# A convolution plus a feed-forward layer on one core: two short tiled matmul steps set in one run, and a third step set in pairs

## The chip, the cores and the metric

The kernel runs on one core of one Trainium2 chip, in float32 and in float32 split into two rounded parts. The metric is the time of one execution in microseconds on the device. The kernel before was timed in three runs, with a median of 1113.24 us.

## The reference, cut to what matters

```python
xn = layernorm(x)                       # x: 2048 positions x 576 channels
# branch A: a long convolution along the positions, one response per channel
P = exp(dt * A * l)                     # l = 0..2047, 128 complex modes per channel
K = real(sum_n C[d,n] * P[d,n,l] * dt[d] * B[d,n])     # the response of channel d
y = irfft(rfft(pad(xn.T)) * rfft(pad(K)))[:2048] + xn * Dskip
# branch B: a feed-forward layer, 576 -> 4608 -> 576
h = silu(xn @ w1)
out = x + y.T + h @ w2
```

The convolution is done as a transform of length 2048 in steps (radix 32, then 64): a first step for the inputs `xn`, the same first step for the responses `K`, a product in the middle, and the way back.

## The kernel before, in words

One generator, `ffn`, issues the feed-forward layer, which is most of TensorE's work: `up` (L313 to L315, tile `ph`) multiplies by `w1`, ScalarE applies silu (`gf`, L321) and rounds (`gh`, L322), VectorE takes the remainder (`gl`, L323); `down` (L338, tile `po`) multiplies by `w2`, and VectorE adds the result to `acc` (L342). Each product is three matmuls of rounded parts.

A second generator, `side`, issues the convolution. `weave` puts its pieces between those of `ffn`: each piece yields a mark, a share of the whole, at which it is due. Within that, a scheduler orders every engine's instructions at build time by priorities, dependencies and free buffers, and the engines then run these fixed orders.

The change is in the stretch of `side` in which the responses are computed (`kgen`, marks 0.13 to 0.597), and the inputs' first step (`spread`) runs beside it.

- `kgen` has 36 chunks of channels. For each, VectorE and ScalarE make tables of sines and cosines (`S`, `C`). At every second chunk a pair is complete. Then TensorE sums the modes into `kp` by 64 small matmuls (L674) which use the array as four column strips of 128x32; ScalarE copies `kp` to `kt` (L681); and TensorE does the first transform step of the same pair by eight matmuls into the two tiles `z` (L689), which use the array as two halves of 64x128. ScalarE copies them into `stage` (L697), and every two pairs SP's queue stores `stage` to `d1k` (L702).
- `spread` has 16 groups of positions and two steps in each. SP's queue loads a group into `xr` (L145). A step rounds half of the rows on ScalarE (`sp`, L150), takes the remainder on VectorE (L151), and does four full 128x128 matmuls in two tiles `pu` (L155, L156), which ScalarE copies to `u1` (L157). POOL's queue stores it to `d1u` (L158). The pool `up` has one buffer of each tile. `side` calls one step after every chunk from the third on.
- `kp`, the two `z` and the `pu` tiles take turns in three PSUM buffers of the pool `pss`.

POOL's queue also loads the later tiles of the feed-forward's input (`xl`, L352; `r4`, L355). After `kgen` an accumulating DMA adds `Dskip` to `d1k` (L705), and the spectral stage (`front`, tiles `pk`, `pu`, `pb`, L804) loads `d1u` and `d1k` (L796).

Of the kernel before, what the change touches and what calls it, by code (L numbers as in the profile page):

```python
# [11 lines left out]
F32 = mybir.dt.float32  # L12
# [7 lines left out]
P = 128  # L20
# [23 lines left out]
def kernel(  # L44
# [21 lines left out]
    nc = tc.nc  # L66
# [14 lines left out]
    d1k = dram.tile([32 * P, D], F32, name="d1k")  # L81
    d2 = dram.tile([32 * P, D], F32, name="d2")
    dxt = [dram.tile([D, 512], F32, name=f"dxt{b}") for b in range(2)]
    dxn = dram.tile([P, NJ, D], F32, name="dxn")
# [6 lines left out]
    f1 = cst.tile([P, P], F32, name="f1")  # L91
# [18 lines left out]
    pss = ctx.enter_context(tc.tile_pool(name="pss", bufs=3, space=PSUM))  # L110
# [25 lines left out]
    def behind(ins):  # L136
        return tc.issue_after(ins) if ins is not None else nullcontext()

    def spread(up):

        s1 = up.tile([P, 2, P], F32R, name="s1", bufs=1)
        nc.gpsimd.dma_start(s1, cs1)
        for j in range(NJ):
            src = up.tile([P, D], F32, tag="xr", name="xr")
            nc.sync.dma_start(src, dxn[:, j])  # L145
            for m in range(2):
                lo, hi = slice(64 * m, 64 * m + 64), slice(64 - 64 * m, 128 - 64 * m)
                u1 = up.tile([P, D], F32, tag="u1", name="u1")
                sp = up.tile([P, D], F32R, tag="sp", name="sp")
                nc.scalar.copy(sp[lo, :], src[lo, :])  # L150
                nc.vector.tensor_sub(sp[hi, :], src[lo, :], sp[lo, :])  # L151
                for h in range(2):
                    hs = slice(h * HD, (h + 1) * HD)
                    pu = pss.tile([P, 512], F32, tag="pss", name="pu")
                    nc.tensor.matmul(pu[:, :HD], s1[:, 0, :], sp[:, hs], start=True, stop=False)  # L155
                    nc.tensor.matmul(pu[:, :HD], s1[:, 1, :], sp[:, hs], start=False, stop=True)  # L156
                    nc.scalar.copy(u1[:, hs], pu[:, :HD])  # L157
                nc.gpsimd.dma_start(  # L158
                    d1u.rearrange("(p m j) d -> m j p d", m=2, j=NJ)[m, j], u1)
                yield j  # L160
# [401 lines left out]
    def kgen():  # L562
        fT, phiT = kf["f"], kf["phi"]
        with tc.tile_pool(name="kg", bufs=1) as kg:
            CH = 8
            NRUN = 4
            NCK = HD // CH
# [50 lines left out]
                return th  # L618

            stage = None  # L620
            tabs = []
            nxt = head(0)
            al = powers(0)
            for i in range(NCK):
                th = nxt
                pk, ak = pw[:, i % 2], al[:, :, i % 2]
                c65 = kg.tile([P, W, 65], F32, tag="c65", name="c65")
                S = kg.tile([P, W, 96], F32, tag="S", name="S", bufs=2)
                C = kg.tile([P, W, 96], F32, tag="C", name="C", bufs=2)
                mag = C  # L630
                nc.scalar.activation(c65, th, AF.Identity, bias=magic)  # L631
                nc.vector.scalar_tensor_tensor(th, c65, MAGIC, th, op0=ALU.subtract, op1=ALU.subtract)  # L632
                nc.scalar.activation(c65, th, AF.Abs)  # L633
                nc.scalar.activation(th, th, AF.Sin, scale=TWO_PI)
                nc.scalar.activation(c65, c65, AF.Sin, scale=-TWO_PI, bias=halfpi)
                for g in range(2):
                    gs = slice(g * CH, (g + 1) * CH)
                    nc.vector.tensor_mul(
                        mag[:, gs, 0:32].rearrange("n d (x y) -> n d x y", y=4),
                        pk[:, gs, 0, :].unsqueeze(3).broadcast_to([P, CH, 8, 4]),  # L640
                        ak[:, g].unsqueeze(2).broadcast_to([P, CH, 8, 4]))
                nc.vector.tensor_mul(
                    mag[:, :, 32:96].rearrange("n d (x y) -> n d x y", y=8),
                    pk[:, :, 1, :].unsqueeze(3).broadcast_to([P, W, 8, 8]),
                    pk[:, :, 2, :].unsqueeze(2).broadcast_to([P, W, 8, 8]))
                if i + 1 < NCK:
                    nxt = head(i + 1)
                    if i % 2 == 1:
                        al = powers(i + 1)
                for dst, t, sg in ((S, th, -1.0), (C, c65, 1.0)):  # L650
                    ov3 = dst.rearrange("n d (x y) -> n d x y", y=32)[:, :, 0:3:2, :]
                    mv3 = mag.rearrange("n d (x y) -> n d x y", y=32)[:, :, 0:3:2, :]
                    nc.vector.tensor_mul(ov3, t[:, :, 0:64].rearrange("n d (x y) -> n d x y", y=32), mv3)
                    nc.vector.scalar_tensor_tensor(dst[:, :, 32:64], t[:, :, 64:32:-1], sg, mag[:, :, 32:64],  # L654
                                                   op0=ALU.mult, op1=ALU.mult)
                tabs.append((S, C))
                if i % 2 == 0:
                    yield (i + 1) / NCK
                    continue

                kp = pss.tile([P, 512], F32, tag="pss", name="kp")
                first = None
                for e in (1, 0):
                    S, C = tabs[e]
                    for gl in range(2):
                        for gp_ in range(2):
                            o = e * 256 + (gl * 2 + gp_) * 64
                            for q in range(4):
                                ch = gp_ * CH + gl * 4 + q
                                dst = kp[32 * q:32 * q + 32, o:o + 64]  # L670
                                begins = e == 1 and gl == 0 and gp_ == 0
                                with tc.high_priority(), behind(None if begins else first):
                                    for n, t in enumerate((C, S)):
                                        mm = nc.tensor.matmul(dst, t[:, ch, :32], t[:, ch, 32:],  # L674
                                                              start=begins and n == 0, stop=True,
                                                              tile_position=(0, 32 * q), skip_group_check=True)
                                if begins:
                                    first = mm.ins
                tabs = []
                kt = kg.tile([P, 512], F32, tag="kt", name="kt")  # L680
                nc.scalar.copy(kt, kp)  # L681

                z = [pss.tile([P, 512], F32, tag="pss", name="z") for _ in range(2)]
                first = None
                for eg in range(4):
                    for h in (1, 0):
                        rows = slice(64 * h, 64 * h + 64)
                        with tc.high_priority(), behind(first):
                            mm = nc.tensor.matmul(z[h][:, eg * P:(eg + 1) * P], kt[rows, eg * P:(eg + 1) * P], f1[rows],  # L689
                                                  start=True, stop=True, tile_position=(64 * h, 0))  # L690
                        first = first or mm.ins
                r = (i - 1) % NRUN
                if r == 0:
                    stage = kg.tile([P, 64, NRUN * CH], F32, tag="stage", name="stage")
                sv = stage[:, :, r * CH:(r + 2) * CH].rearrange("p k (e h c) -> p h e k c", h=2, c=2)
                for h in range(2):
                    nc.scalar.copy(sv[:, h], z[h].rearrange("p (e k c) -> p e k c", e=4, c=2))  # L697
                if r == NRUN - 2:
                    d0 = (i // NRUN) * NRUN * CH
                    kv = d1k.rearrange("(k n) (g d) -> g n k d", n=64, g=2)  # L700
                    for gp_ in range(2):
                        nc.sync.dma_start(kv[gp_, :, :, d0:d0 + NRUN * CH], stage[gp_ * 64:(gp_ + 1) * 64])  # L702
                yield (i + 1) / NCK

        nc.gpsimd.dma_start(d1k.rearrange("(k n) d -> n k d", n=P)[0],  # L705
# [135 lines left out]
    def side():  # L841
# [3 lines left out]
        with tc.tile_pool(name="kf", bufs=1) as kfp:  # L845
# [50 lines left out]
            with tc.tile_pool(name="up", bufs=1) as up:  # L896
                sp = spread(up)
                for n, at in enumerate(kgen()):
                    if n > 1:
                        next(sp, None)  # L900
                    yield marks[0] + at * (marks[1] - marks[0])
                for _ in sp:
                    pass
# [8 lines left out]
        yield from tail()  # L912

    sd = side()
    fg = ffn()
    for g in (sd, fg, sd, sd, fg, sd, fg, sd):
# [84 lines left out]
```

## Time and profile before

| | us |
|---|---|
| median of three runs | 1113.24 (1112.6 to 1115.7) |
| the profiled execution, its own time | 1113.42 |
| its span, first to last instruction | 1111.6 |
| TensorE matmul busy | 1103.3 |
| VectorE busy | 916.9 |
| ScalarE busy | 709.2 |
| GpSimd busy | 69.8 |

The granted TensorE clock was full throughout. In the views, PE is TensorE's matmuls, PEld its weight loads, DVE is VectorE, ACT is ScalarE, POOL is GpSimd and SP the engine that issues most DMAs; a q behind a name is the engine's sequencer or DMA queue. An f32 matmul is recorded twice in the trace, so that a run of 64 matmuls shows as 128 records. In a timeline the first column is the start and the second the duration; matmuls overlap, so that the pitch, from one start to the next, is what a matmul takes of TensorE's time.

### The profile page before, as it was taken

The numbers are of one execution on the slowest core, as the hardware profiler recorded it, in microseconds if no ns is written. First come the engines' busy times: TensorE is split into PE (matmuls) and PEld (weight loads), VectorE is DVE, ScalarE is ACT, GpSimd is POOL, SyncE is SP. The second block draws the span as 40 slices with busy tenths as digits, with TensorE's granted clock in tenths as the row PEclk, the third lists the DMA queues.
The fourth block names the chain that finished last, engine by engine and source line by source line (L and its number), as shares of the span: only waits on it lengthen the run. The fifth ranks groups of instructions, "written<-read, shape, count | busy, mean of one in ns | idle before, by whom it ended". The sixth has DMA issues, their size and how long they took to land.

```text
span 1111.6 us, 22913 instructions
## 1 busy us (share of the span) xinstructions
PE 1103.3 (99%) x9168; PEld 997.8 (90%) x9168; DVE 916.9 (82%) x1546; ACT 709.2 (64%) x1228; POOL 69.8 (6%) x129
## 2 busy tenths in 40 slices
PE   8999999999999999999999999999999999999998
PEld 6998999899889899899989989999999999999887
DVE  6899899999999999999999837787778778784433
ACT  5574456676777676677866536877777878773210
POOL 1100000000000000011000000000000000000111
PEclk9999999999999999999999999999999999999999
DMA  9745522425242515255844163554545445434983
GB/s 258 201 122 152 137 71 61 120 63 130 82 107 80 134 61 131 77 149 161 219 123 105 44 173 106 169 157 128 161 145 150 139 146 171 129 107 130 248 211 86
DMA packets 175563, 148.56 MB, mean 134 GB/s; under 512 B 111024, under 2 KB 142272, under 8 KB 175328
## 3 DMA queue, kind: packets, MB, share of 16 engines
q1 hardware_dynamic: 165136, 112.33, 38.7%
q0 software_dynamic: 9568, 33.62, 9.5%
q8 instruction: 72, 1.18, 0.5%
q10 hardware_dynamic: 752, 1.15, 0.4%
q14 instruction: 35, 0.29, 0.1%
HBM read 102.53 MB, written 44.61 MB: 132 GB/s over the span
## 4 chain that ended last, share of the span: by engine, by line
PE 97%; DMA 1%; DVE 0%; SPq 0%; issue 0%; ACT 0%; ACTq 0%; POOL 0%; DVEq 0%
PE po L338 42%; PE ph L313 35%; PE kp L674 3%; PE ph L314 3%; PE ph L315 3%; PE pu L804 2%; PE pb L804 2%; PE pk L804 2%; PE z L689 2%; PE pu L155 1%; DMA acc<-in_A_u_dram 1%; PE py L825 1%; PE pu L156 1%; DMA w2r<-in_B_w_dram 0%; PE pt L124 0%; DVE st L186 0%
## 5 line engine op out<-in xcount | busy, mean ns | idle before, releaser
L338 PE MATMUL po<-w2l,gh 128*128 128x288 f32 x1152 | 338.5, 295 | 0.9 <-DVE w2l L302 0.9
L338 PE MATMUL po<-w2h,gl 128*128 128x288 f32 x1152 | 336.2, 295 | 0.0
L338 PE MATMUL po<-w2h,gh 128*128 128x288 f32 x1152 | 335.8, 295 | 0.0
L338 PEld LDWEIGHTS po<-w2h,gh 128*128 128x128 f32 x1152 | 215.1, 188 | 7.6 <-issue 2.8
L338 PEld LDWEIGHTS po<-w2l,gh 128*128 128x128 f32 x1152 | 215.9, 188 | 6.1 <-DVE w2l L302 1.1
L338 PEld LDWEIGHTS po<-w2h,gl 128*128 128x128 f32 x1152 | 215.4, 188 | 0.8
L321 ACT ACTIVATE gf<-ph 128x512 f32<-128x512 f32 (+1 forms) x148 | 86.4, 585 | 142.9 <-PE ph L315 128.3
L313 PE MATMUL ph<-xh,w1h 128*128 128x512 f32 (+1 forms) x592 | 162.1, 388 | 1.2 <-ACT gf L321 1.2
L313 PE MATMUL ph<-xl,w1h 128*128 128x512 f32 (+1 forms) x592 | 161.4, 386 | 0.0
L313 PE MATMUL ph<-xh,w1l 128*128 128x512 f32 (+1 forms) x592 | 161.0, 385 | 0.0
L342 DVE TENSOR_TENSOR acc<-po,acc 128x288 f32<-128x288 f32 x288 | 126.4, 452 | 37.4 <-PE po L338 36.1
L323 DVE TENSOR_TENSOR gl<-gf,gh 128x512 fp32r<-128x512 f32 (+1 forms) x148 | 99.2, 673 | 64.8 <-ACT gh L322 64.1
L313 PEld LDWEIGHTS ph<-xh,w1l 128*128 128x128 f32 x592 | 108.1, 188 | 19.9
L313 PEld LDWEIGHTS ph<-xl,w1h 128*128 128x128 f32 x592 | 108.0, 188 | 20.0 <-DVE xl L126 0.2
L313 PEld LDWEIGHTS ph<-xh,w1h 128*128 128x128 f32 x592 | 104.5, 188 | 18.5 <-ACT gf L321 1.8
L322 ACT CAST gh<-gf 128x512 fp32r<-128x512 f32 (+1 forms) x148 | 89.8, 609 | 10.1 <-PE po L338 7.1
L631 ACT ACTIVATE c<-th,magic 128x1040 f32<-128x1040 f32 x36 | 42.1, 1169 | 37.9 <-DVE C L654 28.0
L633 ACT ACTIVATE c<-th 128x1040 f32<-128x1040 f32 x36 | 38.7, 1075 | 34.0 <-DVE th L632 34.0
L300 ACT CAST w2h<-w2r 128x576 fp32r<-128x576 f32 x72 | 46.9, 671 | 17.2 <-PE po L338 14.9
L282 DVE TENSOR_TENSOR w1l<-w1r,w1h 128x640 fp32r<-128x640 f32 x72 | 57.1, 818 | 0.2
L314 PE MATMUL ph<-x,w1h 128*128 128x512 f32 (+1 forms) x148 | 57.0, 385 | 0.0
L315 PE MATMUL ph<-x,w1l 128*128 128x512 f32 (+1 forms) x148 | 56.9, 385 | 0.0
(184 smaller groups left out, 1830.1 us busy)
## 6 DMA issues: line engine op xcount, KB each, us to landing
w2r<-in_B_w_dram SPq DMA_DIRECT2D x72, 288.0 KB, 3.7
w1r<-in_B_w_dram SPq DMA_DIRECT2D x35, 512.0 KB, 3.9
d1u<-u POOLq DMA_DIRECT2D x32, 288.0 KB, 2.6
d1k<-stage SPq DMA_DIRECT2D x18, 512.0 KB, 6.8
ur<-d1u SPq DMA_DIRECT2D x32, 288.0 KB, 3.9
kr<-d1k SPq DMA_DIRECT2D x32, 288.0 KB, 2.8
d<-yo POOLq DMA_DIRECT2D x32, 288.0 KB, 3.7
ys<-d SPq DMA_DIRECT2D x32, 288.0 KB, 11.6
```

The lines of the kernel that those rows point to most:

```text
L282: pins["w1l"] = nc.vector.tensor_sub(l1, src, h1).ins
L300: pins["w2h"] = nc.scalar.copy(h2, r2).ins
L313: nc.tensor.matmul(ph, w[:, kt, :], v[:, kt, a:e], start=n + kt == 0, stop=False)
L314: nc.tensor.matmul(ph, h1[:, 4, :], x4[:, a:e], start=False, stop=False)
L315: pins["pe"] = nc.tensor.matmul(ph, l1[:, 4, :], x4[:, a:e], start=False, stop=True).ins
L321: nc.scalar.activation(gf, ph, AF.Silu)
L322: pins["gh"] = nc.scalar.copy(gh, gf).ins
L323: pins["gl"] = nc.vector.tensor_sub(gl, gf, gh).ins
L338: pins["pe"] = nc.tensor.matmul(po[:, :HD], G[blk, t][g][:, js], W2[half, c, t][w][:, hs], start=n == 0, stop=n == 3 * FT - 1).ins
L342: nc.vector.tensor_add(acc[j][:, hs], po[:, :HD], acc[j][:, hs])
L631: nc.scalar.activation(c65, th, AF.Identity, bias=magic)
L804: nc.tensor.matmul(dst, st, mv[:, hs], start=n == 0, stop=n == 3 * len(terms) - 1)
```

## The change

The first transform step of a pair is taken out of the loop's body into a function, `along`, and is issued one pair later, straight behind the next pair's `kp` matmuls; the last pair's is issued at the end. `kt` gets two buffers, since it lives one pair longer. `spread` is called twice after every chunk of even number from the third on, that is after a chunk that makes tables alone, instead of once after each. The loads of `xr` go to POOL's queue instead of SP's.

```diff
         for j in range(NJ):
             src = up.tile([P, D], F32, tag="xr", name="xr")
-            nc.sync.dma_start(src, dxn[:, j])
+            nc.gpsimd.dma_start(src, dxn[:, j])
...
+            kts = []
+            def along(first):
+                nonlocal stage
+                i, kt = kts.pop(0)
+                z = [pss.tile([P, 512], F32, tag="pss", name="z") for _ in range(2)]
+                for eg in range(4):
+                    for h in (1, 0):
+                        rows = slice(64 * h, 64 * h + 64)
+                        with tc.high_priority(), behind(first):
+                            mm = nc.tensor.matmul(z[h][:, eg * P:(eg + 1) * P], kt[rows, eg * P:(eg + 1) * P], f1[rows],
+                                                  start=True, stop=True, tile_position=(64 * h, 0))
+                        first = first or mm.ins
+                ...
+                for h in range(2):
+                    nc.scalar.copy(sv[:, h], z[h].rearrange("p (e k c) -> p e k c", e=4, c=2))
+                ...
...
                 tabs = []
-                kt = kg.tile([P, 512], F32, tag="kt", name="kt")
+                if kts:
+                    along(mm.ins)
+                kt = kg.tile([P, 512], F32, tag="kt", name="kt", bufs=2)
                 nc.scalar.copy(kt, kp)
-                z = ...        # the same matmuls, copies and stores, for this pair's own kt
+                kts.append((i, kt))
+                if i + 1 == NCK:
+                    along(None)
                 yield (i + 1) / NCK
...
                 for n, at in enumerate(kgen()):
-                    if n > 1:
+                    if n % 2 == 0 and n:
+                        next(sp, None)
                         next(sp, None)
                     yield marks[0] + at * (marks[1] - marks[0])
```

More of the change, by code (lines that the diff above doesn't have):

```diff
@@ L620, in kgen @@
             stage = None
+            kts = []
[10 more added lines that the diff above has]
+                        first = first or mm.ins
+                r = (i - 1) % NRUN
+                if r == 0:
+                    stage = kg.tile([P, 64, NRUN * CH], F32, tag="stage", name="stage")
+                sv = stage[:, :, r * CH:(r + 2) * CH].rearrange("p k (e h c) -> p h e k c", h=2, c=2)
+                for h in range(2):
+                    nc.scalar.copy(sv[:, h], z[h].rearrange("p (e k c) -> p e k c", e=4, c=2))
+                if r == NRUN - 2:
+                    d0 = (i // NRUN) * NRUN * CH
+                    kv = d1k.rearrange("(k n) (g d) -> g n k d", n=64, g=2)
+                    for gp_ in range(2):
+                        nc.sync.dma_start(kv[gp_, :, :, d0:d0 + NRUN * CH], stage[gp_ * 64:(gp_ + 1) * 64])
             tabs = []
@@ L679, in kgen @@
                 tabs = []
-                kt = kg.tile([P, 512], F32, tag="kt", name="kt")
+                if kts:
+                    along(mm.ins)
+                kt = kg.tile([P, 512], F32, tag="kt", name="kt", bufs=2)
                 nc.scalar.copy(kt, kp)
[L683 to L702, printed above, removed]
+                kts.append((i, kt))
+                if i + 1 == NCK:
+                    along(None)
                 yield (i + 1) / NCK
```

## The prediction

> **What bounds the kernel now.** I read the page's totals first, then who TensorE waited for, then the stretch that the change touches.
>
> ```profile
> span 1111.6 us, 22913 instructions
> ...
> PE 1103.3 (99%) x9168; PEld 997.8 (90%) x9168; DVE 916.9 (82%) x1546; ACT 709.2 (64%) x1228; POOL 69.8 (6%) x129
> ...
> PE 97%; DMA 1%; DVE 0%; SPq 0%; issue 0%; ACT 0%; ACTq 0%; POOL 0%; DVEq 0%
> ```
>
> The first two lines are totals, the third the chain that ended last. TensorE is on the chain for 97% of the span. The next lines are everything that the matmuls waited for in the whole run, and then the busy time of the engines in the stretch of `kgen`.
>
> ```profile
> PE pz L857 <- DVE zero L852: 1.3, 1, 1.3
> PE ph L313 <- ACT gf L321: 1.2, 3, 0.5
> PE po L338 <- DVE w2l L302: 0.9, 1, 0.9
> PE pt L124 <- DVE xn L195: 0.2, 1, 0.2
> ```
>
> ```profile
> core 0: us, PE busy (x) PEld busy (x) DVE busy (x) ACT busy (x) POOL busy (x), PEclk, DMA share, GB/s
> 180.00:640.00 460.00, 460.00 (x4859) 415.67 (x4860) 441.98 (x661) 317.03 (x477) 21.53 (x39) 1.00 0.41 109
> ```
>
> Waits come to 3.6 us, none of them in this stretch: there PE is busy for 460.00 of 460.00 us at full clock. So nothing that other engines or queues save can show in the time here; only a shorter stream of matmuls can. DVE is busy for 441.98 of 460, close behind.
>
> Busy is not the same as useful, though. The starts of matmuls show what it costs to go between the full array, the four strips of `kp` and the two halves of `z`. First into and out of a run of `kp`, then of `z`:
>
> ```profile
> 169.88 0.29 PE L338 MATMUL po<-w2h,gh 128*128 128x288 f32 x1
> 170.01 0.29 PE L338 MATMUL po<-w2l,gh 128*128 128x288 f32 x1
> 170.23 0.27 PE L674 MATMUL kp<-C 128*32 128x64 f32 x3
> ...
> 172.07 0.22 PE L674 MATMUL kp<-S 128*32 128x64 f32 x1
> 172.22 0.54 PE L338 MATMUL po<-w2h,gl 128*128 128x288 f32 x2
> 172.60 0.29 PE L338 MATMUL po<-w2h,gh 128*128 128x288 f32 x1
> ```
>
> ```profile
> 177.15 0.39 PE L315 MATMUL ph<-x,w1l 128*128 128x512 f32 x1
> 177.37 0.39 PE L313 MATMUL ph<-xh,w1h 128*128 128x512 f32 x1
> 177.69 0.38 PE L689 MATMUL z<-f,kt 64*128 64x128 f32 x2
> ...
> 178.57 0.28 PE L689 MATMUL z<-f,kt 64*128 64x128 f32 x2
> 178.78 0.40 PE L155 MATMUL pu<-sp,s 128*128 128x288 f32 x1
> 179.02 0.30 PE L156 MATMUL pu<-sp,s 128*128 128x288 f32 x1
> ```
>
> A `po` follows a `po` after 0.13 us, but the first `kp` follows after 0.22: 0.09 more. From `ph`, 0.32 instead of 0.22 to 0.23: again 0.09. On the way out the first full matmul starts 0.15 behind the last `kp`, and the one behind it 0.11 late: 172.22 to 172.60 is 0.38 for two where 0.26 is usual, and directly at 178.78 to 179.02, 0.24 for 0.13. The first matmuls of `z` take 0.38 where its last take 0.28: 0.10 for a weight load that nothing hides.
>
> **The change, part by part.**
>
> *One run instead of two.* Before there are 18 runs of `kp` (1152 records of `C`, 64 to a run, and as many of `S`) and 18 of `z` (288, 16 to a run), with full matmuls between all of them:
>
> ```profile
> L674 PE MATMUL kp<-C 128*32 128x64 f32 x1152 | 35.2, 222 | 0.0
> ...
> L689 PE MATMUL z<-f,kt 64*128 64x128 f32 x288 | 20.9, 285 | 0.0
> ```
>
> In the changed program as built, 17 runs of `kp` are followed at once by the eight `z` matmuls of the pair before; the number of matmuls of each kind is the same. Two things are new: the last pair's `z` follows 9 `up` matmuls later and is cut into four and four, with 4 `up` matmuls between.
>
> For one merge, before: 0.15 out of `kp`, 0.11 for the late second matmul, and 0.09 into `z`, 0.35 us in all; after: one direct step from `kp` to `z`. No row of before shows that step. Its bounds are `kp`'s own pitch, as if nothing had to be switched (170.23 to 172.07 is 1.84 us for 127 steps: 0.015), and the 0.22 from `po` into `kp`. I take 0.15, from `kp` to `po`: the same run has to end, and what comes next is another division of the array in either case. A merge then saves 0.35 - 0.15 = 0.20 us (0.13 to 0.335), and 17 save 3.4 us (2.2 to 5.7). The unhidden first load of `z` stays, since it is inside the run.
>
> The Trainium skill, TensorEngine Tiling (Array Packing), section Tiling Modes, says that changing the mode, and not merely the tile, drains the engine. By that rule strips to halves drains as strips to full does, and the sum goes by 0.15; the 0.09 on every way in agrees with it, and no run of before shows strips to halves.
>
> The cut of the last `z` adds one way out and one way in: at the cut 0.20 (178.58 to 178.78) for a mean pitch of some 0.06 to 0.10, so +0.10; then 0.11, 0.09 and the 0.10 of a first load: +0.40 us.
>
> *ScalarE's copies behind the merged run.* A run now holds all three `pss` buffers, and the first `pu` after it needs one back.
>
> ```profile
> L681 ACT COPY kt<-kp x18: 561/572/588, 172.5 to 640.5; 128x512 f32<-128x512 f32 x18
> ```
>
> `kp`'s buffer comes free first, 0.57 us after ScalarE gets to it, while the `z` part of the run still takes 178.78 - 177.69 = 1.1 us. In the built order at least 14 full matmuls (2 `up`, 12 `down`: 2.0 us) stand between a run and the next `pu`. So ScalarE may be 1.1 + 2.0 - 0.6 = 2.5 us late at no cost; with ACT busy for 317 of 460 us I cost this at nothing. If that cover were gone it is paid once a run.
>
> *The steps of `spread` in pairs.* Their matmuls are full ones and keep their pitch wherever they stand. But `u1` has one buffer, so the second step's copy waits on ScalarE until the first step's store has landed. Behind it on ScalarE stand `gf` and `gh`, for which TensorE waits.
>
> ```profile
> L158 POOL DMA_DIRECT2D d1u<-u x32: 539/539/577, 183.8 to 628.3; - x32
> DMA to landing us min/median/max: 2.4/2.6/5.6
> ```
>
> In the built order ScalarE has 3.0 to 3.4 us of other work between the two steps' copies in three of the sixteen pairs, 4.0 to 4.4 in five, more in the others (before: 4.0 at least). That covers a landing of 2.6 us. Cost nothing; without the cover up to 5.6 - 3.0 = 2.6 us in a pair.
>
> *The loads on POOL's queue.*
>
> ```profile
> L145 SPq DMA_DIRECT2D xr<-dxn x16: 326/333/808, 137.1 to 583.4; - x16
> SPq L145 <- DVE sp L151: 76.9, 13, 11.8
> POOL xl L352 <- PE ph L313: 9.1, 2, 5.0
> L362 ACT CAST xh<-xl x8: 615/622/633, 506.2 to 546.1; 128x512 fp32r<-128x512 f32 x8
> ```
>
> SP loses 16 issues of 0.33 us and 76.9 us in which the weights' loads stood behind a load that waited for `sp`. As matmuls wait for no load in this stretch, the gain is nothing. POOL gains 16 issues of about 0.54 (as for `d1u`), 8.6 us beside 21.5 in the 460. A load waits for the second step's `sp` and stands ahead of that step's own store, which can't be ready earlier. The second load of `xl` gets one such load ahead of it; some 25 instructions of ScalarE lie between that and its first use at L362, so nothing again; at most a few us, once. A load that lands some 3 us after issue has most of a pair's time, (640 - 180)/16 = 29 us, ahead of its use.
>
> *The end of `kgen`.* The last `z` leads to the store, to the DMA that adds `Dskip`, to the loads of the spectral stage:
>
> ```profile
> 656.93 0.86 POOL L705 DMA_DIRECT2D d1k<-in_A_Dskip_dram  x1 [28.09 <-DMA d1k<-stage]
> 662.76 0.32 SPq L796 DMA_DIRECT2D kr<-d1k  x1
> 673.38 0.67 ACT L790 CAST kh<-kr 128x576 fp32r<-128x576 f32 x1
> 646.34 1.20 PE L313 MATMUL ph<-xh,w1h 128*128 128x512 f32 x4
> kr<-d1k SPq DMA_DIRECT2D x32, 288.0 KB, 2.8
> ```
>
> From the end of `z` (646.34) to landed data it took 662.76 + 2.8 - 646.34 = 19.2 us. In the built order 58 `up` and 107 `down` matmuls, 58 x 0.227 + 107 x 0.133 = 27.4 us, now lie between the last `z` and the first `pk` (79 and 100 before, 31.2 us). 8 us are left for the splits; nothing.
>
> **Sum.** -3.4 + 0.4 = -3.0 us against the profiled execution's own 1113.42 us, whose span is 1111.6: 1110.4. The median of the runs is 0.2 lower, so 1110.2 us, 0.27% less. A measurement of this kernel tells about 0.3%, 3.3 us, from no change: 1109.9 is the border.
>
> **Rivals.** *No switch from strips to halves.* At 0.015 a merge saves 0.335, in all 5.7 - 0.4 = 5.3 us: 1107.9. For it: both divide the array, and small matmuls follow each other at 0.015. Against: the drain on each way in.
>
> *The saving is eaten by small waits.* The built orders differ everywhere in this stretch, DVE is at 96%, and one late `gl`, `w2l` or table in a few places gives 1 to 4 us: 1111 to 1114. Against it: in the order of before, made in the same way, not one matmul waited here.
>
> *Slower: ScalarE stands for the store.* Where `d1u` lands after 5.6 us instead of 2.6, ScalarE stands for 1.2 to 2.6 us in the eight close pairs, with `gf` behind it. If half of 2.6 reaches TensorE, 8 x 1.3 = 10 us: 1120. It decides the sign from 3.0/8 = 0.4 us a pair, and counts as slower from 6.3/8 = 0.8 us a pair. For it: one buffer, a maximum of 5.6. Against: the median, and that TensorE keeps two `ph` tiles. The Trainium skill, SBUF — State Buffer, section SBUF: two separate sides, says that a DMA issued from POOL can stand still for want of descriptors while VectorE runs certain copies; with DVE busy throughout, the 2.6 us of the stores against 2.9 of SP's `xr` do not bear it out.
>
> **Chances.** Forecast 0.57, no switch 0.14, small waits 0.13, slower 0.16. Faster by over 0.3% is the second and, as the forecast ends 0.3 us short of the border and its step is known to 0.05 us a merge at best, a third of the first: 0.14 + 0.19 = 0.33. Within 0.3%: the rest of the first and the third, 0.38 + 0.13 = 0.51. Slower: 0.16. The range from 1107.9 to 1115.0 holds the first three and the mild part of the last.
>
> **What would show it.** In the profile after: the step from `kp` to `z` at 0.15 us; 17 fewer late second matmuls; PE still without waits from 180 to 640; first `pk` some 3 us earlier against the same start. A wait of TensorE on `gf` behind L157, or of L157 on a DMA, would be the slower rival; a step of 0.02 the faster one. I am wrong if TensorE's busy share of that stretch falls, or if the time moves while the starts around the merged runs don't.

## The result, and the profile after

The changed kernel takes 1120.02 us (median of six runs, 1116.49 to 1121.28) against 1113.64 for the kernel before in the same batch (1112.6 to 1116.53): a ratio of 1.0052, with a 95% interval from 1.0041 to 1.0063. It is slower by 0.5%; the forecast was 1110.2 and the range ended at 1115.0. The profiled execution took 1119.51 us.

The page's totals and its chain:

```profile
span 1117.7 us, 22950 instructions
...
PE 1104.0 (99%) x9168; PEld 1001.1 (90%) x9168; DVE 916.7 (82%) x1546; ACT 706.2 (63%) x1228; POOL 78.8 (7%) x145
...
PE 74%; DVE 11%; issue 6%; DMA 4%; ACT 3%; SPq 1%; POOL 0%; DVEq 0%; POOLq 0%; ACTq 0%
```

The same work is done by as many matmuls, but TensorE has fallen from 97% of the chain to 74%: the end now hangs on other engines in between. What the matmuls waited for, in the whole run, and then the stretch of `kgen`:

```profile
PE po L338 <- ACT w2h L300: 4.3, 3, 2.9
PE ph L313 <- ACT gf L321: 1.6, 3, 0.9
PE pz L868 <- DVE zero L863: 1.3, 1, 1.3
PE py L836 <- DMA ys<-d: 1.2, 1, 1.2
PE ph L313 <- ACT w1h L280: 0.5, 1, 0.5
```

```profile
180.00:640.00 460.00, 455.07 (x4723) 413.47 (x4722) 438.20 (x655) 313.96 (x476) 29.14 (x53) 1.00 0.41 109
```

PE was busy for all of the 460 us; now 4.9 us of them are empty, and most of that is one line that was not in the list before: `po` waits for `w2h`, the rounded copy of a row of `w2`. (`w2r` is such a row as loaded, in two buffers; `py` is the last stage, which loads the spectral stage's result back as `ys`; `acc` holds the sums of the feed-forward, which are stored to `dr` at the end of the first half.)

**Where the 6.1 us of span came from.** From the starts of all matmuls after the first 40 us I took off each pitch what is usual for its kind (0.133 us for `po` and `pu`, 0.227 for `ph`, 0.0145 for `kp`, 0.059 for `z`) and sorted what was left over. "Stand still" is a rest of over 0.15 us between full matmuls or where a switch took longer than a switch does; "slow" a rest of 0.06 to 0.15 us.

| us, whole run | before | after |
|---|---|---|
| late second matmul behind a run | 4.68 | 2.96 |
| full matmul to `z` | 1.63 | 0.18 |
| `kp` to full | 2.42 | 0.13 |
| `kp` to `z` | 0.00 | 2.29 |
| `z` to full | 2.57 | 2.71 |
| within `z` | 0.09 | 1.03 |
| stand still | 0.00 | 7.21 |
| slow | 0.70 | 2.48 |

The first six rows are the merge with the cut of the last `z`: 2.1 us less. The last two are 9.0 us more, and 0.8 us less is in small rests, the start and the end: -2.1 + 9.0 - 0.8 = 6.1.

The step from `kp` to `z` in the timeline (start, duration, engine, line):

```profile
564.24 0.31 PE L701 MATMUL kp<-S 128*32 128x64 f32 x6
564.48 1.16 PE L633 MATMUL z<-f,kt 64*128 64x128 f32 x16
565.57 0.50 PE L314 MATMUL ph<-x,w1h 128*128 128x512 f32 x1
565.91 0.39 PE L315 MATMUL ph<-x,w1l 128*128 128x512 f32 x1
```

Six records of `kp` begin 0.24 us ahead of the first `z`, five pitches of about 0.015 and one long one: 0.149 us here as in all 17 merges. The second full matmul behind the run is 0.11 us late (565.57 to 565.91 is 0.34 where 0.23 is usual), as before.

Inside `z` the 17 merged runs keep the pitches of before: 0.89 us from the first start to the last. The whole rise of "within `z`" is the last pair's `z`, which is cut in two. TensorE's timeline there, and ScalarE's:

```profile
652.62 1.16 PE L633 MATMUL z<-f,kt 64*128 64x128 f32 x8
653.71 0.50 PE L313 MATMUL ph<-xh,w1h 128*128 128x512 f32 x1
654.83 1.16 PE L633 MATMUL z<-f,kt 64*128 64x128 f32 x8
```

```profile
653.81 0.63 ACT L641 COPY stage<-z 128x512 f32<-128x512 f32 x1 [0.52 <-PE z L633]
```

Eight records take as long here as sixteen at 564.48. In a whole run two records start 0.007 us apart and the next two 0.105 us later; in the cut parts every record starts 0.112 us behind the one before. ScalarE copies the first tile out before the second part begins, so each part is one tile, that is one half of the array: what the two halves did beside each other is done one after the other, and the row rises by 0.94 us.

**The largest stand still.** TensorE's timeline right behind that run:

```profile
566.67 0.29 PE L338 MATMUL po<-w2h,gl 128*128 128x288 f32 x1
569.81 0.51 PE L338 MATMUL po<-w2h,gh 128*128 128x288 f32 x1 [2.85 <-ACT w2h L300]
570.11 0.44 PE L338 MATMUL po<-w2l,gh 128*128 128x288 f32 x1
570.35 0.44 PE L338 MATMUL po<-w2h,gl 128*128 128x288 f32 x1
```

ScalarE's, up to the copy that TensorE waits for, and SP's queue:

```profile
558.40 1.17 ACT L658 ACTIVATE c<-th,magic 128x1040 f32<-128x1040 f32 x1
569.09 0.67 ACT L300 CAST w2h<-w2r 128x576 fp32r<-128x576 f32 x1 [9.51 <-DMA w2r<-in_B_w_dram]
```

```profile
557.80 0.34 SPq L345 DMA_DIRECT2D dr<-acc  x1
562.17 1.71 SPq L168 DMA_DIRECT2D acc<-in_A_u_dram  x4
563.99 6.92 SPq L291 DMA_DIRECT2D w2r<-in_B_w_dram  x3
```

ScalarE stands for 9.51 us until the first of these loads of `w2r` has landed, at 569.06, and it is issued only at 563.99. Two things hold it. Its buffer comes free when VectorE has taken the remainder of an earlier row:

```profile
561.78 1.43 DVE L302 TENSOR_TENSOR w2l<-w2r,w2h 128x576 fp32r<-128x576 f32 x2
```

The first of the two ends at 562.54. And ahead of the load on SP's queue stand four loads of `acc`, which wait until the store of the old `acc` (557.80) has landed; they hold it for 1.45 us more. The landing takes another 5.1 us. The wait has a second price: behind it `po` follows `po` after 0.24 us instead of 0.133. The windows show why (last three columns: granted clock, DMA share, GB/s):

```profile
570.00:571.00 1.00, 1.00 (x5) 1.00 (x5) 1.00 (x3) 1.00 (x2) 0.00 (x0) 0.50 0.00 0
573.00:574.00 1.00, 1.00 (x8) 1.00 (x8) 1.00 (x2) 1.00 (x3) 0.00 (x0) 0.82 0.17 36
574.00:575.00 1.00, 1.00 (x8) 0.92 (x8) 0.46 (x2) 1.00 (x4) 0.00 (x0) 1.00 0.00 0
```

The clock is halved for about 3.4 us (three at 0.50 and a third of the fourth), which loses some 1.7: nearly the whole rise of "slow".

### The profile page after: what moved, and what is told of

It reads as the page before. It is cut to its first block, busy times and chain, and to the rows that moved or that the text cites. A ratio compares the mean times of both kernels' runs of the same rounds, so it can differ in the third digit from the quotient of the medians.

```text
span 1117.7 us, 22950 instructions
## 1 busy us (share of the span) xinstructions
PE 1104.0 (99%) x9168; PEld 1001.1 (90%) x9168; DVE 916.7 (82%) x1546; ACT 706.2 (63%) x1228; POOL 78.8 (7%) x145
## 4 chain that ended last, share of the span: by engine, by line
PE 74%; DVE 11%; issue 6%; DMA 4%; ACT 3%; SPq 1%; POOL 0%; DVEq 0%; POOLq 0%; ACTq 0%
PE po L338 32%; PE ph L313 27%; PE ph L314 2%; PE ph L315 2%; PE pu L815 2%; PE pk L815 2%; PE pb L815 2%; PE kp L701 2%; DMA w2r<-in_B_w_dram 2%; DVE C L669 1%; DVE S L680 1%; DVE acc L342 1%; PE z L633 1%; DVE C L680 1%; PE py L836 1%
## 5 line engine op out<-in xcount | busy, mean ns | idle before, releaser
L302 DVE TENSOR_TENSOR w2l<-w2r,w2h 128x576 fp32r<-128x576 f32 x72 | 53.6, 750 | 5.7 <-ACT w2h L300 5.6
```

What stands on the lines that cost most here:

```text
L302: nc.vector.tensor_sub(l2, r2, h2)
```

## The experiments

Two readings stood against each other. One is that a single mishap, the loads of `w2r` behind those of `acc` on SP's queue, made the loss. The other is that every engine runs an order fixed at build time, that the order of before happens to have no stand still, and that any displacement deals new orders with waits of their own.

| run | what it is | median us | ratio to before (95%) | stand still, us |
|---|---|---|---|---|
| before | | 1113.3 to 1113.7 | 1 | 0.00 |
| after | the change | 1120.02 | 1.0052 (1.0041 to 1.0063) | 7.21 |
| e1 | merge alone | 1119.32 | 1.0050 (1.0038 to 1.0062) | 6.91 |
| e2 | pairs alone | 1118.12 | 1.0043 (1.0027 to 1.0059) | 5.95 |
| e3 | POOL's loads alone | 1113.96 | 1.0000 (0.9991 to 1.0009) | 1.19 |
| e4 | merge and pairs | 1125.06 | 1.0109 (1.0085 to 1.0133) | 11.21 |
| e6 | merge and POOL's loads | 1120.65 | 1.0064 (1.0051 to 1.0077) | 10.28 |
| e5 | change, `acc` loads on POOL | 1119.64 | 1.0053 (1.0038 to 1.0069) | 8.63 |
| e11 | e5, a tail mark later | 1115.81 | 1.0024 (1.0014 to 1.0034) | 5.99 |
| e7 | before, `spread` a chunk later | 1118.89 | 1.0053 (1.0041 to 1.0065) | 4.12 |
| e9 | before, `spread` a chunk earlier | 1117.10 | 1.0035 (1.0021 to 1.0048) | 3.45 |
| e10 | before, mark 0.600 | 1120.44 | 1.0067 (1.0054 to 1.0080) | 4.61 |
| e14 | before, mark 0.594 | 1116.16 | 1.0026 (1.0017 to 1.0034) | 1.85 |
| e8 | change, mark 0.62 | 1126.26 | 1.0116 (1.0103 to 1.0129) | 14.81 |
| e12 | merge, `kt` first on ScalarE | 1131.93 | 1.0167 (1.0147 to 1.0186) | 18.12 |
| e13 | e11, `w2r` loads on POOL | 1125.05 | 1.0108 (1.0094 to 1.0122) | 9.21 |
| e15 | e11, mark 0.594 | 1116.02 | 1.0024 (1.0015 to 1.0033) | 3.91 |
| e16 | e15, `dr` stores on POOL | 1116.45 | 1.0025 (1.0014 to 1.0036) | 4.03 |
| e17 | e11, `dr` stores on POOL | 1117.02 | 1.0030 (1.0019 to 1.0042) | 6.07 |

The last column is worked out from the profiled execution, which in e2, e5 and e6 took 2.0, 2.6 and 3.2 us more than the median. A `ph` at half clock rests 0.2 us and so counts as stand still here: 1.4 us of the column in e6 and in e13, 1.6 in e8, 2.2 in e12, nothing in the others.

### The parts by themselves

**e1, the merge alone:** `along`, `kt` in two buffers; `spread` and the loads as before.

```diff
+                if kts:
+                    along(mm.ins)
+                kt = kg.tile([P, 512], F32, tag="kt", name="kt", bufs=2)
```

> Only the first part of the change: the z matmuls straight behind the next pair's kp, kt with two buffers; the inputs' steps and their loads as before. Theory 1 (the merge saves 17 x 0.20 - 0.40 = 3.0 us, and the loss of the whole change is weights' loads, w2r, that stand on SP's queue behind the reload of acc): here one of the three w2r loads stands ahead of that reload, so 1113.6 - 3.0 = 1110.6, ratio 0.997, no wait on w2h above 1 us. Theory 2 (the pairs of input steps bunch work on VectorE and ScalarE, so that results come late): also 0.997. Theory 3 (loads on POOL's queue come late): also 0.997. If the merge itself is what costs: above 1.000.

Slower by 0.50%. The switches cost the same 2.1 us less as in the whole change, and 6.9 us of stand still outweigh it; so neither the pairs nor POOL's loads are needed for the loss. Its first wait is new, for `kt`:

```profile
PE pu L155 <- ACT kt L710: 3.4, 4, 1.3
PE ph L313 <- ACT gf L321: 2.4, 4, 1.1
```

One of the four, on ScalarE and on TensorE:

```profile
388.63 1.16 ACT L658 ACTIVATE c<-th,magic 128x1040 f32<-128x1040 f32 x1 [2.08 <-DVE th L617]
389.70 0.61 ACT L322 CAST gh<-gf 128x512 fp32r<-128x512 f32 x1
390.21 1.35 ACT L280 CAST w1h<-w1r 128x640 fp32r<-128x640 f32 x2
391.47 1.07 ACT L660 ACTIVATE c<-th 128x1040 f32<-128x1040 f32 x1
392.44 0.56 ACT L710 COPY kt<-kp 128x512 f32<-128x512 f32 x1
```

```profile
391.48 0.29 PE L338 MATMUL po<-w2h,gh 128*128 128x288 f32 x1
393.05 0.40 PE L155 MATMUL pu<-sp,s 128*128 128x288 f32 x1 [1.28 <-ACT kt L710]
```

`kp` is complete at about 388.4, and its copy stands behind a table step that waits 2.08 us for VectorE, and behind what follows. It begins over 4 us late; the prediction's cover was 2.5.

**e2, the pairs alone:**

```diff
-                    if n > 1:
+                    if n % 2 == 0 and n:
+                        next(sp, None)
                         next(sp, None)
```

> Only the second part: two input steps after every chunk of even number; z matmuls and loads as before. Theory 1: one of the three w2r loads stands ahead of the reload of acc, so within 1 us of before, ratio 0.999 to 1.001. Theory 2: the bunching is there in full without the merge's saving, so +8 us or so, ratio 1.007. Theory 3: 1.000.

Slower by 0.43%. Waits of 2.4 us on `w2h` and 2.6 on the loads of `ys` in the tail; `u`'s copies wait for a store once, for 0.3 us.

**e3, POOL's loads alone:**

```diff
-            nc.sync.dma_start(src, dxn[:, j])
+            nc.gpsimd.dma_start(src, dxn[:, j])
```

> Only the third part: the xr loads on POOL's queue. Theory 1: two of the three w2r loads stand ahead of the reload, ratio 1.000. Theory 2: 1.000. Theory 3: +8 us or so, ratio 1.007, with ScalarE waiting for xr.

No change to 0.1%, as the prediction had it for this part.

**e4, merge and pairs without POOL's loads:** the change with that line undone.

> The change without its loads on POOL's queue. In the order as built all three w2r loads stand behind the second reload of acc, as in the changed kernel. Theory 1: as the changed kernel, ratio 1.004 to 1.006, with a wait of 2 to 4 us on w2h some 565 us into the span and the clock at half for 3 to 4 us behind it. Theory 2: also 1.004 to 1.006, but with waits spread over many places. Theory 3: 0.997.

1125.06: 5.0 us more than the whole change, with the same orders of TensorE and ScalarE but for two rows. ScalarE's `sp` waits 11.8 us for `xr` here and 4.4 in the whole change. The part that is worth nothing alone is worth 5 us beside the others; that the loads come late on SP because the two steps of a pair now stand close together is a reading, and no run parts it from the chance of the order.

**e6, merge and POOL's loads:**

> The merge with the xr loads on POOL's queue, the input steps after every chunk as before. The order of TensorE and ScalarE is that of the merge alone; SP's queue has no xr loads to stand behind. Theory A: the part of the merge's loss that goes through w2r goes with them (0.7 us of waits on w2h), about 1118.5; the waits of pu on kt stay. Theory B: as the merge alone, 1119.3.

1120.65, and 10.3 us of stand still where e1 with nearly the same orders has 6.9: the queue alone moves the waits about (4.1 us on `w2h` here, 0.7 in e1). In the medians the two are 1.3 us apart.

### One mishap, or any order

**e5, the loads of `acc` taken out of SP's queue:**

```diff
-                    acc[7 + j], acc[8 + j] = load_x(7 + j, accp, "acc", (nc.sync,))
+                    acc[7 + j], acc[8 + j] = load_x(7 + j, accp, "acc", (nc.gpsimd,))
```

> The changed kernel with one line more: the four reloads of acc in the last chunk of the first half go to POOL's queue, so that no w2r load stands behind them on SP's. The orders of TensorE and ScalarE are the same as in the changed kernel, instruction by instruction. Theory A (w2r loads that stand on SP's queue behind waiting instructions bring w2h late, and each long stand still of TensorE is followed by some 3.6 us of half clock): the stand still of 2.85 us near 567 us and the half clock behind it go, 2.85 + 1.8 = 4.65 us less than the changed kernel, about 1115.4. Theory B (VectorE, busy for 96% of this stretch, is late, and SP's queue only passes that on): within 1 us of the changed kernel, 1120.

The orders of TensorE and ScalarE are those of the changed kernel, instruction by instruction. The stand still at 567 falls from 2.85 to 0.04 us and the half clock behind it is gone. But the load of `w2r` is issued at 563.48, only 0.5 us sooner than in the changed kernel and 0.03 us after VectorE's `w2l`, which comes later here; the rest is its landing, 3.3 us where it was 5.1. So the reading holds for a part of that wait at most. For the time it fails: 1119.64.

```profile
PE py L836 <- DMA ys<-d: 4.3, 1, 4.3
PE ph L313 <- ACT gf L321: 1.6, 4, 0.5
PE po L338 <- ACT w2h L300: 1.6, 1, 1.6
```

What was saved at 567 is waited for at 1042, where the first `py` needs data that go out and come back: TensorE comes there 2.4 us sooner than in the changed kernel, and the data come 0.6 us later (first `py` at 1042.19 for 1041.55). The single mishap falls as the cause of the total.

**e11, the first `py` later:** e5 and

```diff
-        tail_at = (0.91, 0.934, 0.967, 0.0072)
+        tail_at = (0.91, 0.94, 0.967, 0.0072)
```

> The changed kernel with acc's reloads on POOL's queue and the last stage's first mark at 0.940 for 0.934, so that some 6 us more of full matmuls stand between the last pb and the first py; else TensorE's order is that of the changed kernel. Theory A, carried to the tail (a py that waits for ys has simply been put too close behind the spectral stage): the wait of py goes, 1.2 to 4.3 us with half clock behind it, 1115 to 1117. If the tail is bound by its transfers: the wait comes back at a later py, 1119 to 1120.

1115.81: no wait on `ys` any more, and 4.2 us less than the changed kernel. The later mark without e5's line was not run, so what each is worth by itself stays open. Still 0.24% slower than before, with 3.6 us on `w2h`, and one of these waits is again the one at 567, though up to there TensorE's and ScalarE's orders and SP's queue are those of e5:

```profile
568.07 0.40 PE L338 MATMUL po<-w2h,gh 128*128 128x288 f32 x1 [1.72 <-ACT w2h L300]
```

The load is issued at 563.04, again 0.03 us after `w2l`, and lands 4.3 us later. So e5's 0.04 us hung on a quick landing, and with the loads of `acc` out of the way VectorE's `w2l` says when the load starts.

**e7 and e9, before with `spread` one chunk later and one earlier.** Nothing of the change is in them.

```diff
-                    if n > 1:
+                    if n > 2:      # e7;  e9: n > 0
```

> The kernel before with its input steps begun one chunk later (n > 2 for n > 1), all else the same: neither merge nor pairs nor other queues. Theory C (the order of before has no wait because it is the fitted one, and any displacement of the steps brings waits of some us): 1117 to 1121, with stand stills of TensorE in the stretch of kgen. Theory D (the pairs and the merge themselves make the waits): 1113.6, ratio 1.000.

> The kernel before with its input steps begun one chunk earlier (n > 0 for n > 1). Theory C (any displacement of the steps deals the orders anew and brings waits, as in the kernel whose steps begin one chunk later): 1116 to 1121, one to three stand stills. Theory E (beginning later was bad by itself, since the steps then end later): 1113.5 or less.

Slower by 0.53% and 0.35%. In e7, TensorE and the copy that it waits for:

```profile
441.85 0.29 PE L338 MATMUL po<-w2h,gl 128*128 128x288 f32 x1
444.51 0.85 PE L338 MATMUL po<-w2h,gh 128*128 128x288 f32 x2 [2.37 <-ACT w2h L300]
445.15 0.44 PE L338 MATMUL po<-w2l,gh 128*128 128x288 f32 x1
445.39 0.44 PE L338 MATMUL po<-w2h,gl 128*128 128x288 f32 x1
```

```profile
443.78 0.67 ACT L300 CAST w2h<-w2r 128x576 fp32r<-128x576 f32 x1 [3.69 <-DMA w2r<-in_B_w_dram]
```

The same wait and the same half clock as in the changed kernel (0.24 from `po` to `po`), without merge, pairs or POOL's loads.

**e10 and e14, before with the end of `kgen` 0.5% later and earlier:**

```diff
-        marks = (0.13, 0.597, 0.823)
+        marks = (0.13, 0.600, 0.823)      # e10;  e14: 0.594
```

> The kernel before with kgen's end mark at 0.600 for 0.597, 0.3% of the run; all steps the same, in the same places among the chunks. Theory C: 1116 to 1121. Theory E: within 1 us of before.

> The kernel before with kgen's end mark at 0.594 for 0.597, the mirror image of the mark at 0.600. In the order as built, 89 down and 56 up matmuls stand between the last pb and the first py (before 71 and 56, changed kernel 50 and 50). Theory C: waits in the stretch of kgen again, but none of py: 1115 to 1119. If only the later place of the spectral stage cost: 1113.3 or less.

Slower by 0.67% and 0.26%. So four neutral displacements of before, two each way, cost 2.5 to 7.2 us, and the whole change, with its 2.1 us of saving, costs 6.4, which lies inside that range. e3, which moves a queue and leaves the orders as they were but for one matmul, costs nothing. The second reading holds, for the four displacements that were run.

### Trying for an order without waits

**e8, the change with the end of `kgen` much later** (`marks` 0.62 for 0.597):

> The changed kernel with kgen's end mark at 0.62 for 0.597, so that the same work of VectorE is spread over 545 us for 519 of the run. Theory B: VectorE's share falls from 96% to 92%, the waits shrink to under 2 us, and the merge's saving of 2 us shows: 1111 to 1114. Theory A: still waits on w2h, 1116 to 1121. Theory C: anything between 1113 and 1122, by the new order.

**e12, the merge with `kt` ahead of the table step on ScalarE:**

```diff
-                nc.scalar.activation(c65, th, AF.Identity, bias=magic)
+                with behind(pins.get("kt")):
+                    nc.scalar.activation(c65, th, AF.Identity, bias=magic)
...
-                nc.scalar.copy(kt, kp)
+                pins["kt"] = nc.scalar.copy(kt, kp).ins
```

> The merge alone, with the first table operation of a chunk put behind the copy of kt on ScalarE, so that kt no longer stands behind a table that waits for VectorE. If the waits of pu on kt were that (3.4 us in four places of the merge alone): they go, 1119.3 - 3.4 = 1116, unless the new order brings others (theory C): 1116 to 1121.

In e12 no `pu` waits for `kt` any more, as meant. And in the stretch itself, up to 665 us, both come near to what was sought: the stand still there is 1.20 us in e8 and 1.41 in e12 (5.90 in the changed kernel, 6.91 in e1), with no wait on `w2h`. Yet both are the slowest of all, for 13.6 and 16.7 us of stand still in the tail. SP's queue in e8, from 1015 to 1050:

```profile
SPq L267 <- DMA d<-yo: 39.7, 1, 39.7
```

The last loads of `w1` stand behind the landing of the spectral stage's last result (45.1 us in e12). They are issued at 1016.4 in before, at 1038.8 in e8 and at 1042.6 in e12, and `w1h` is then late by 7.4 and 9.4 us: an order in which the spectral stage ends later moves these loads too.

**e13, e11 with the loads of `w2r` on POOL's queue:**

```diff
-            pins["load"] = nc.sync.dma_start(r2, w2v[:, c * FT + t, :]).ins
+            pins["load"] = nc.gpsimd.dma_start(r2, w2v[:, c * FT + t, :]).ins
```

> The changed kernel with acc's reloads on POOL's queue and the later first mark of the last stage (1115.8 us, with 3.6 us of stand stills on w2h left and a like amount of slow clock and small waits), and now the w2r loads on POOL's queue too, where less stands ahead of them. Theory A: the waits on w2h go and the merge's 2 us show: 1110 to 1112, ratio 0.998. Theory C: the loads' other queue deals part of the order anew, 1114 to 1119.

1125.05. It loses 5 us at the start, in a stretch that was not meant (the first stand still in `kgen`, at 231.6 in e11, is at 236.9 here):

```profile
18.36 0.74 PE L313 MATMUL ph<-xh,w1h 128*128 128x256 f32 x4 [2.66 <-ACT gf L321]
```

and in `kgen` still stands for 2.9 us on `w2h` and 1.8 on `acc`. So it says little on the question.

**e15, e11 with the mark of e14:**

> The changed kernel with acc's reloads on POOL's queue, the later first mark of the last stage and kgen's end mark at 0.594. Theory C: dealt anew against the kernel with 0.597, 1112 to 1119, with other stand stills in other places. Theory A: as that kernel or better, 1114 to 1116, its waits on w2h.

1116.02, the time of e14 without the change (1116.16), though e15 stands still for 2.1 us more (3.91 against 1.85). This is the nearest that the runs come to the saving in the time: it pays for just so much waiting. The two differ in the queue of `acc`'s loads and in the tail's mark as well, so this is a sum that fits and no proof.

**e16 and e17, e15 and e11 with the stores of `acc` on POOL's queue too:**

```diff
-                nc.sync.dma_start(dr0[rows, :], acc[j])
+                nc.gpsimd.dma_start(dr0[rows, :], acc[j])
```

> The kernel of e15 with the stores of acc to dr (L345) on POOL's queue instead of SP's as well. The orders of TensorE, ScalarE and VectorE are the same as in e15, instruction by instruction; only SP's and POOL's queues differ. In e15 TensorE still stood for 1.4 us on w2h and 3.9 us in all, and SP's queue showed the loads of w2r behind three dr stores that took 13 us of waiting (547.4 to 560.5). Theory (waits of the fixed orders eat the saving of 2.1 us, and the part on w2h hangs on SP's queue): the w2h waits go, the time falls by 1 to 1.5 us to 1114.5 to 1115, still above before's 1113.4, since some 2 us of other waits stay. Rival (what is won at one wait comes back at the next): no change, 1116.0. Other risk: a dr store on POOL waits for acc ahead of a d1u store, ScalarE then stands for the one buffer of u1: 2 to 6 us slower, with a wait of L157 on a DMA in the trace.

> The kernel of e11 with the stores of acc to dr (L345) on POOL's queue instead of SP's as well; here the built orders of TensorE and ScalarE differ from e11's throughout. Theory that every new order deals its own waits: 1113 to 1119, not to be told ahead within that, against 1115.8 for e11. Rival (the waits come from the loads of w2r behind acc and dr on SP's queue alone): no w2h wait, no stand still in 180 to 640, 1112 or less.

1116.45 and 1117.02: no gain. In e16 the orders of TensorE, ScalarE and VectorE are those of e15, and in e15 two loads of `w2r` stood behind three of these stores, which SP issued over 13 us as they waited for `acc`. With the stores gone, the load is issued no sooner (561.3 against 560.8). VectorE's, SP's, ScalarE's and TensorE's lines in e16:

```profile
560.52 1.42 DVE L302 TENSOR_TENSOR w2l<-w2r,w2h 128x576 fp32r<-128x576 f32 x2
```

```profile
561.30 2.57 SPq L291 DMA_DIRECT2D w2r<-in_B_w_dram  x2
```

```profile
565.81 0.67 ACT L300 CAST w2h<-w2r 128x576 fp32r<-128x576 f32 x1 [1.14 <-DMA w2r<-in_B_w_dram]
```

```profile
566.53 0.40 PE L338 MATMUL po<-w2h,gh 128*128 128x288 f32 x1 [1.01 <-ACT w2h L300]
```

and what the loads of `w2r` wait for on SP from 180 to 640:

```profile
SPq L291 <- DVE w2l L302: 118.4, 19, 20.2
```

`w2r` has two buffers, and a buffer is free when VectorE has taken the remainder `w2l`. VectorE's own fixed order, in a stretch where it is busy for 95% of the time, says when that is; one place of `w2l` behind other work becomes, a load later, a wait of TensorE. In e15 and in e16 the load is issued 0.03 us after the end of `w2l`. The queue added to that at one place, the 1.45 us at 567 in the changed kernel.

No version beats before. Open stays whether the merge would show as a gain in an order without waits; none of the orders that were run is one. The nearest untried one is e8 with the tail's marks and the last loads of `w1` set to suit its later spectral stage. A third buffer for `w2r`, which would part TensorE from the place of `w2l`, was not tried: there is no room for it in SBUF.

## Why the prediction was wrong, point by point

**Right: what bounds the kernel, and the step from `kp` to `z`.** TensorE sets the time, and the step was put at 0.15 us with bounds of 0.015 and 0.22; it is 0.149 in all 17. The Trainium skill, TensorEngine Tiling (Array Packing), section Tiling Modes, has a change of mode drain the engine; strips to halves at the price of strips to full agrees with it.

**Right: what a merge saves. Mis-sized: the cut of the last `z`.** 3.0 us were forecast, 2.1 came. A merge saves 0.135 us out of `kp` and 0.107 at the late second matmul and 0.091 into `z`, and pays 0.135 for the step (each beyond the usual pitch): 0.20 a merge and 3.4 in all, as worked out. The cut was put at +0.40 and costs 1.3: 0.34 for one more way in, way out and late matmul, and 0.94 within `z`. The prediction priced the cut as a switch and took the pitch inside the parts as unchanged; but each part is one half alone, and its records follow each other at 0.112 us where a whole run has 0.059 in the mean.

**Wrong: "I cost this at nothing".** This is the step that failed, and it was taken four times: for ScalarE's copies, the pairs, the loads and the end of `kgen`. Its ground stands in the rival that was put at 0.13: "in the order of before, made in the same way, not one matmul waited here". That was read as slack. But it was a property of one order. e7, e9, e10 and e14 are made in the same way too, and wait. The rival "the saving is eaten by small waits" named the mechanism and priced it at 1 to 4 us; measured are 7.2 us of standing and 1.8 of slow clock, 9.0, and the second term was not thought of at all. One of the prediction's own signs of being wrong is there: TensorE is busy for 455.07 of the 460 us.

**The covers, one by one.** ScalarE's 2.5 us for `kt`: not enough in e1, where the copy was 3.4 to 4.9 us late four times; in the whole change no `pu` waited for it. The landing of `d1u`: covered, no copy of `u` waited on a DMA, so the slower rival as described falls, though its 1120 is the time that came. The loads on POOL's queue: nothing by themselves (e3), but worth 5.0 us beside the pairs (e4), which the prediction left out, since it weighed each part against the order of before. The end of `kgen`: no matmul waited for `kr`; but how far the tail's first loads lie behind the spectral stage decides waits of up to 4.3 us on `ys` (e5) and 9.4 on `w1h` (e12), and that was not looked at.

**What would have shown it.** VectorE at 96% was named, as the engine that is close behind. Two rows of the waits of before, of SP's queue and of ScalarE from 180 to 640, say more:

```profile
SPq L291 <- DVE w2l L302: 38.1, 18, 11.5
```

```profile
ACT w2h L300 <- DMA w2r<-in_B_w_dram: 2.1, 3, 1.7
```

The loads of `w2r` waited for VectorE 18 times, and ScalarE for a load already in three places. A chain VectorE, load, ScalarE, TensorE, with two buffers and nearly full at its head, has little room for a new order. Whether more time for VectorE gives it room is not parted: in e8, which gives it, the stand still of the stretch is 1.20 us, but e12, without it, has 1.41.

## What to carry to other kernels

Where a build fixes each engine's order, "this engine never waits" describes that order and is no slack; before a gain of a few us is forecast, the same kernel with a mark moved by half a per cent tells what a mere new order costs (here 2.5 to 7.2 us, more than the gain). A wait that is removed shows in the time only if TensorE doesn't reach the next late thing sooner, so look one wait further down the run, the tail above all. And follow a late load past its queue to what frees its buffer.

## What was not expected of the hardware

A stand still of TensorE of 2 to 3 us can cost half as much again. Behind 2.85 us (after) and 2.37 us (e7) the granted clock was 0.50, with 0.24 us from `po` to `po`, for about 3.4 us. Behind 1.64 us in e6 it was halved as well; behind 1.58 us in e5, 1.72 in e11 and 2.08 in e4 it was not, so that the length alone doesn't decide. The Trainium skill, TensorE: Matmul & The Clock Gate, section HAM oscillation — how this bites in real kernels, asks for no gaps over some 3.4 us; the traces here show halving behind shorter ones, and where they differ the traces decide.

Two halves of the array, given matmuls by turns, did eight 64x128 matmuls in the time that four of one half took: 0.89 us from the first start to the last in both cases (564.48 and 652.62 after). Setting one half's four behind the other's doubled the time.
